# Highway FFN behind a gated recurrence: small PSUM slots for the last units, one product e for fifteen middle units, and a new order

## The chip, the core and the metric

The kernel runs on one core of a Trainium2 chip. Its engines are named as in the profile: PE (matmul), DVE (vector), ACT (activation), POOL (GpSimd) and SP, which here only starts transfers. The metric is the device time of one execution in microseconds; lower is better.

## The reference

A gated recurrence over time runs along each of 4 sequences of 6336 steps with 256 channels, and its output goes through a highway layer token by token:

```python
sig = 1.0 / (1.0 + np.exp(-f_logit))
f = lower_bound + (1.0 - lower_bound) * sig
h = f[:, t] * h + (1.0 - f)[:, t] * x[:, t]        # y[:, t] = h
...
H = np.maximum(y @ w_h, 0.0)
T = 1.0 / (1.0 + np.exp(-(y @ w_t + b_t)))
out = T * H + (1.0 - T) * y
```

All inputs and the output are float32; there are 25344 tokens (x, f_logit and the output are 26 MB each).

## The kernel before

The 25344 tokens are cut into 28 units (`parts`): two of 2 blocks of 128 tokens, one of 4, twenty-three of 8, one of 4 and one of 2. Each unit passes through a chain of steps, most of them done twice, once for each half of 128 channels. The order in which all steps of all units are issued is written out by hand as a string of tokens (lines 49 to 98). A token such as `s12.1:0` is a step (s), a unit (12), a half or part (1) and a buffer slot (0); a trailing `v` puts a step on DVE that else runs on POOL (b, e) or ACT (f, c). Every engine works through its own instructions in the order of the string, and waits by semaphores for what it reads and for a slot to be free. So an instruction that waits holds up all that stands behind it on its engine, SP's queue of transfers too.

The steps of a unit, with their engine and line:

- l, x (SP, 237): load the logits and x of the unit, 128 partitions by tokens by channels.
- u (ACT, 249): u = sigmoid(-logit), in fp16.
- b (POOL or DVE, 257): bv = u * x, in two parts, written so that two tokens make one 32-bit word.
- i (PE, 264): transposes of u into PSUM; f (ACT or DVE, 275 or 273): f = 1 + ncc * u of one half, with channels on partitions.
- p (PE, 284): transposes of bv as 32-bit words into PSUM.
- s (DVE, 301): the recurrence of one half as one scan along the tokens; it starts from the last value of the unit before, so all scans of a half run one after the other.
- z, g (PE, 313 and 115): the two matrix products of the highway layer for one half of the outputs; each reads both halves of y. t (ACT, 326): sigmoid of z. d (DVE, 330): d = max(ncc * y, g), which stands for the relu, shifted.
- e (POOL or DVE, 336): d = d * t, in parts: for a unit of 8 blocks the first half whole (1024 elements a partition) and the second in two parts of 512. A part needs d and t of the half it lies in.
- o (PE, 349 and 350): for four blocks of tokens, a product with diag and one with the identity transpose y and d back and add them; it reads both halves of d, so o.0 needs e.0 and e.1, and o.1 needs e.0 and e.2.
- c (ACT or DVE): copy of the result from PSUM; w (SP, 364): its transfer to memory.

WT, WH and dg (DVE) scale the weights and make the diagonal matrices; k is a number of idle matmuls on zeros (`k*4:1`: four, in slot 1).

PSUM has two kinds of slots. `one_bank` gives a0 and a1, one bank each, for the transposes i and p. `two_banks` gives three slots of two banks, b0 to b2, for z, g, o and k. `shared` makes every b or e on POOL wait for the b or e (or weight scaling) on DVE that was issued last before it.

Of the kernel before, what the change touches and what calls it, by code (L numbers as in the profile page):

```python
# [53 lines left out]
x7:1 f4.0:0 c1.0:1 g2.1:1 z2.0:0 p3.1:1 i4.1:0 g2.0:2 d2.1:0 s3.1 u5:0 t2.0 d2.0 f4.1:1 b4.0 w1.0 k*4:1 e2.0v e2.1v
z3.1*1:1 p4.0:1 i5.1:0 t3.1:1 b5.0:1 f5.1:2 o2.0:0 c2.0:2 w2.0 b5.1 l8:2 x8:2 g3.1:1 p4.1:0 l12:3 l10:4 z3.0:2 s4.0:1
u6:1 i5.0:1 f5.0:0 g3.0:0 x12:0 i6.1:1 x9:3 t3.0 l11:5 d3.1:0 f6.1:3 u7:0 s4.1 e3.1 p5.0:0 d3.0 z4.1:1 g4.1:0 s5.0:2
p5.1:1 i6.0:0 d4.1:1 g4.0:2 t4.1:0 f6.0:0 u9:2 z4.0:0 k*4:1 b6.1:0 i7.1:0 b6.0 e3.0 e3.2 s5.1 d4.0 b7.0:1 p6.1:1
o3.0:1 g5.1:2 t4.0 x10:4 f7.1:1 c3.0:0 w3.0 s6.1:3 i7.0:0 b7.1 z5.1:0 f7.0:2 k*4:1 d5.1:2 t5.1:1 p6.0:0 e4.1v u8:0
e4.0v o3.1:1 o4.0:0 c3.1:1 p7.1:1 z5.0:2 e5.1 g5.0:1 w3.1 c4.0:2 w4.0 t5.0 e4.2 s6.0 s7.1:0 b8.1:0 i8.1:0 z6.0:0 d5.0
f8.1:0 p7.0:1 o4.1:2 u12:1 i9.1:0 s7.0 t6.0:0 e5.2 c4.1:3 w4.1 g6.1:1 i8.0:1 u10:3 d6.1:0 g7.1:0 f8.0v:1 l27:0 z7.0:1  # L60
b8.0 p8.0:1 e5.0 t7.0:1 d7.1:1 x11:1 f9.1:2 s8.0:1 z6.1:2 g6.0:0 g7.0:1 t6.1 b12.1:1 d7.0 d6.0 i9.0:0 p8.1:1 u11:0
z7.1:2 k*4:1 b9.0:2 f9.0:1 t7.1 o5.1:1 b9.1 i11.1:0 c5.1:0 w5.1 b10.0:0 o5.0:0 f11.1:3 s8.1 c5.0:1 z8.0:2 p9.0:1 w5.0
l13:1 e7.1v g8.1:1 e6.0v i10.1:0 t8.0:2 e6.2v f10.1:0 o6.1:0 z8.1:2 e6.1v e7.0v s9.0:2 e7.2 c6.1:2 w6.1 p9.1:0 i12.1:1
t8.1 f12.1:1 o7.1:0 c7.1:3 b12.0 g8.0:2 b10.1 d8.1:2 s9.1 o7.0:1 d8.0 p10.1:1 i10.0:0 w7.1 s10.1:0 o6.0:0 e8.1 g9.0:2
u27:2 c7.0:0 f10.0:2 c6.0:1 u13:3 b11.0:2 g9.1:1 d9.0:0 p10.0:0 s10.0 w7.0 i11.0:1 b11.1 f11.0:0 z9.1:0 t9.1:0 e8.2
e8.0 z9.0:2 t9.0 i12.0:1 d9.1 f12.0:2 p11.1:0 z10.0:0 t10.0:1 e9.0 g10.0:1 l15:0 u15:0 o8.1:2 p11.0:1 s11.1:3 c8.1:0
d10.0:1 o8.0:0 c8.0:2 e9.2 e9.1v g10.1:1 i13.0:0 x15:0 o9.0:2 w6.0 x13:2 e10.0v f13.0:3 b15.0:0 z10.1:0 c9.0:1 p12.0:0
t10.1 s11.0 d10.1 i13.1:1 b15.1 z11.1:2 g11.1:1 s12.0:1 f13.1:0 t11.1:0 b13.0:2 i15.0:1 f15.0:2 l14:2 e10.1 u14:1
b13.1 p12.1:0 o9.1:0 c9.1:3 g11.0:2 i15.1:1 e10.2 l17:3 d11.1:2 s12.1 z11.0:1 t11.0 f15.1:1 x14:3 p13.0:0 z12.1:0
t12.1:1 g12.1:1 u17:0 d11.0 p13.1:1 w8.0 o10.0:2 z12.0:0 e11.1 s13.0:2 d12.1:0 b14.1:1 o10.1:1 c10.0:2 i14.0:0 g12.0:2  # L70
s13.1 b14.0 w8.1 t12.0 i14.1:1 w9.0 e11.0v w9.1 g13.0:0 c10.1:0 l16:0 e11.2v z13.0:1 x16:0 d12.0 f14.0:0 f14.1:3
d13.0:1 p14.0:0 t13.0:0 o11.1:2 s14.0:0 u16:1 l18:1 c11.1:1 e12.2 z13.1:0 p14.1:1 o11.0:1 p15.0:0 s14.1 c11.0:3 t13.1
z14.1:2 s15.0:3 g13.1:1 x17:1 d13.1 t14.1:2 g14.1:0 d14.1:2 i16.0:1 z14.0:2 e12.0 e12.1 p15.1:0 e13.0 b16.0:1 s15.1
u18:3 b16.1 w10.0 o12.0:1 f16.0:0 i16.1:1 g14.0:0 t14.0 d14.0 c12.0:2 b17.0:2 b17.1 w10.1 e13.1v f16.1:2 w11.1 o12.1:2
c12.1:0 z15.1:1 e14.0v w11.0 p16.0:0 s16.0:1 e14.2 i17.1:1 o13.0:0 t15.1:1 g15.1:1 f17.1:1 p16.1:1 d15.1:0 z15.0:2
s16.1 l20:0 c13.0:1 i18.0:0 g15.0:0 d15.0 e13.2 o13.1:1 e14.1 e15.2 u20:1 f18.0:0 x18:2 t15.0 i17.0:0 f17.0:2 b18.1:0
w12.0 p17.1:1 o14.0:2 l19:1 s17.1:2 g16.0:0 c13.1:2 p17.0:0 d16.0:1 b18.0 s17.0 o14.1:1 i18.1:1 u19:0 c14.1:3 g16.1:0
d16.1 w12.1 f18.1:1 c14.0:0 z16.1:1 t16.1:0 p18.1:1 s18.1:0 i19.0:0 z17.1:2 x20:0 e15.1 l22:2 g17.1:0 e15.0 d17.1:2
x19:1 b20.0:1 g17.0:1 f19.0:2 d17.0 b20.1 t17.1:1 b19.0:2 i19.1:0 z17.0:2 p18.0:1 u22:3 w13.1 f19.1:1 w13.0 b19.1
w14.1 s18.0 e17.1v t17.0 e17.0v o15.0:0 w14.0 e17.2 o15.1:1 c15.0:1 x22:2 i20.1:0 z16.0:2 f20.1:3 l21:0 p19.0:1 t16.0  # L80
e16.0 c15.1:0 z18.0:0 s19.0:3 b22.0:0 e16.1 b22.1 p19.1:0 o17.0:2 t18.0:1 o17.1:1 c17.0:2 i20.0:1 x21:3 g18.0:0 e16.2
s19.1 f20.0:0 c17.1:3 u21:0 b21.1:2 l23:1 g19.0:2 p20.1:0 d18.0:0 b21.0 i22.0:1 g19.1:0 f22.0:1 d19.0:2 s20.1:2
z19.0:1 d19.1 w15.1 z19.1:2 i21.0:1 p20.0:0 t19.0:2 g18.1:1 s20.0 t19.1 u23:1 w17.1 d18.1 e19.0v o16.0:0 c16.0:0 e19.1
o16.1:2 i21.1:0 f21.0:0 w15.0 f21.1:2 g20.1:0 d20.1:1 e18.0v z18.1:1 e19.2 w17.0 c16.1:1 i22.1:1 x23:0 f22.1:3 p21.1:0
o19.0:0 l24:2 t18.1 z20.1:2 b23.1:1 e18.1 e18.2 b23.0 p21.0:1 c19.0:2 o19.1:1 w16.0 t20.1:0 w16.1 e20.2 s21.1:1 s21.0
g20.0:0 c19.1:3 i23.0:0 x24:1 f23.0:2 z20.0:2 t20.0 e20.1 p22.1:1 d20.0 e20.0 z21.0:1 t21.0:1 u24:0 i23.1:0 g21.1:0
w19.0 o18.0:2 s22.1:3 c18.0:0 b24.0:2 w19.1 f23.1:0 p22.0:1 d21.1:2 b24.1 z21.1:1 t21.1 e21.2 s22.0 x25:2 g21.0:0
o18.1:2 c18.1:1 p23.0:0 d21.0 i24.1:1 s23.0:0 z22.1:1 f24.1:1 g22.1:0 l25:0 o20.0:2 e21.0 t22.1:0 p23.1:0 d22.1:0
i24.0:1 e21.1 c20.0:2 f24.0:2 o20.1:1 c20.1:3 u25:0 b25.1:0 g22.0:0 w18.0 s23.1 p24.0:1 w18.1 d22.0 l26:1 s24.0:2
z22.0:2 w20.0 z23.0:1 b25.0 t22.0 o21.1:0 p24.1:0 t23.0:1 c21.1:0 g23.1:2 i25.0:1 e22.2 s24.1 o21.0:1 f25.0:0 g23.0:0  # L90
d23.1:1 i25.1:0 d23.0 c21.0:1 p25.0:1 z23.1:1 s25.0:1 g24.1:2 u26:1 f25.1:1 t23.1 z24.1:0 e22.0 i26.1:0 d24.1:2 e22.1
w20.1 o22.1:1 x27:0 t24.1:2 c22.1:2 p25.1:1 o22.0:0 x26:1 b26.1:1 f26.1:0 c22.0:3 g24.0:2 i26.0:0 z24.0:1 s25.1 w21.1
b26.0 p26.0:1 e23.2 w21.0 f26.0:2 d24.0 z25.0:0 p26.1:0 e23.0 z25.1:2 t24.0 s26.0:3 s26.1 g25.1:1 t25.0:0 b27.0:0
# [311 lines left out]
```

## Time and profile before

| | |
|---|---|
| median of three runs | 210.59 us (209.63 to 212.25) |
| profiled execution | 211.79 us, of which the span from first to last instruction is 209.6 us |
| granted PE clock, mean | 0.998 |
| busy, of the span | PE 93%, DVE 93%, ACT 92%, POOL 83% |
| moved by DMA | 78.67 MB, mean 375 GB/s |

Busy time is the time in which an engine had an instruction in work. Matmuls overlap, so a busy PE isn't PE at its peak. In a row of the timeline stand start, duration, engine, line and operation, and in brackets the idle time before it with what ended it. In a row of groups stand the number of instructions, their busy time together, the mean of one in ns, and the idle time before them. Neighbouring instructions overlap at their ends by about 0.1 us, so the distance from start to start is what one costs in a full stretch.

### The profile page before, as it was taken

What the parts mean: (1) busy time and instruction counts of PE and PEld (TensorE: products, weight loads), DVE (VectorE), ACT (ScalarE), POOL (GpSimd) and SP (SyncE); (2) the same over time, 40 slices, a digit from 0 to 9 for tenths busy, and PEclk for the clock granted to TensorE, in tenths of its full rate; (3) what the DMA queues carried; (4) which work ended last, traced back from release to release, by engine and by line L of the source; (5) the groups of instructions that cost most, each with busy time, mean ns of one, the idle gap of its engine ahead of it and who ended that gap; (6) DMA issues with size and microseconds to landing.
All of it is one profiled execution on the core that took longest, in us unless ns stands there. A gap on an engine that the chain in (4) does not pass through costs nothing. (4 is left out here: it accounts for less than half of the span.)

```text
span 209.6 us, 4674 instructions
## 1 busy us (share of the span) xinstructions
PE 194.3 (93%) x1852; PEld 135.3 (65%) x1852; DVE 194.5 (93%) x167; ACT 192.8 (92%) x187; POOL 173.1 (83%) x114
## 2 busy tenths in 40 slices
...
GB/s 197 400 431 419 417 414 422 417 424 410 422 410 420 376 368 336 428 422 415 413 417 422 419 410 425 406 430 425 404 427 375 371 374 377 308 106 200 103 358 292
DMA packets 15980, 78.67 MB, mean 375 GB/s; under 512 B 1748, under 2 KB 2264, under 8 KB 10072
## 3 DMA queue, kind: packets, MB, share of 16 engines
...
## 5 line engine op out<-in xcount | busy, mean ns | idle before, releaser
L257 POOL TENSOR_TENSOR bv<-u,x 128x1024 bf16<-128x1024 f16 (+1 forms) x50 | 101.9, 2059 | 17.4 <-ACT u L249 8.0
L301 DVE TENSOR_TENSOR_SCAN y<-f,y,bT 128x1024 bf16<-128x1024 f16 (+5 forms) x54 | 106.9, 1990 | 1.8 <-ACT t L326 1.0
L336 POOL TENSOR_TENSOR d<-d,t 128x512 bf16<-128x512 bf16 (+2 forms) x53 | 71.4, 1364 | 12.9 <-DVE d L336 10.2
L330 DVE SCALAR_TENSOR_TENSOR d<-y,ncc,g 128x1024 bf16<-128x1024 bf16 (+2 forms) x56 | 63.2, 1137 | 2.3 <-PE g L313 1.3
L326 ACT ACTIVATE t<-z,bt 128x1024 bf16<-128x1024 f32 (+2 forms) x56 | 58.4, 1058 | 2.0 <-PE z L313 1.0
L275 ACT ACTIVATE f<-uT,ncc 128x1024 f16<-128x1024 f16 (+2 forms) x51 | 55.5, 1097 | 1.0 <-PE uT L264 1.0
L249 ACT ACTIVATE u<-l 128x2048 f16<-128x2048 f32 (+2 forms) x28 | 49.0, 1750 | 6.9 <-DMA l<-in_f_logit_dram 6.9
L359 ACT COPY o<-op 128x1024 f32<-128x1024 f32 (+1 forms) x50 | 50.7, 1025 | 2.2 <-PE op L350 2.2
L349 PE MATMUL op<-diag,y 128*128 128x128 f16 x396 | 49.4, 219 | 0.7 <-DVE d L330 0.6
L350 PE MATMUL op<-ident_b,d 128*128 128x128 bf16 x396 | 49.4, 219 | 0.1
L350 PEld LDWEIGHTS <-d 128*128 128x128 bf16 x396 | 44.1, 113 | 3.3 <-POOL d L336 0.7
L349 PEld LDWEIGHTS <-y 128*128 128x128 bf16 x396 | 44.2, 113 | 2.0
L313 PE MATMUL g<-y,w_sb 128*128 128x512 bf16 (+1 forms) x112 | 39.5, 367 | 1.2 <-ACT o L359 0.7
L313 PE MATMUL z<-y,w_sb 128*128 128x512 bf16 (+1 forms) x112 | 39.4, 367 | 1.0 <-DVE y L301 0.8
L115 PE MATMUL z<-y,w_sb 128*128 128x512 bf16 x92 | 34.9, 379 | 0.0
L115 PE MATMUL g<-y,w_sb 128*128 128x512 bf16 x92 | 34.9, 379 | 0.0
L284 PE MATMUL bT<-ident_f,bv 128*128 128x128 f32 x198 | 31.5, 276 | 3.4 <-POOL bv L257 1.4
L264 PE MATMUL uT<-ident_h,u 128*128 128x128 f16 x396 | 30.8, 219 | 3.7 <-ACT f L275 1.9
L264 PEld LDWEIGHTS <-u 128*128 128x128 f16 x396 | 25.9, 98 | 11.7 <-issue 4.9
L313 PEld LDWEIGHTS <-w_sb 128*128 128x128 f16 x224 | 21.5, 98 | 15.7 <-issue 0.9
L284 PEld LDWEIGHTS bT<-ident_f,bv 128*128 128x128 f32 x198 | 22.9, 141 | 12.4 <-POOL bv L257 2.5
L115 PEld LDWEIGHTS <-w_sb 128*128 128x128 f16 x184 | 18.0, 98 | 17.2 <-issue 3.1
...
## 6 DMA issues: line engine op xcount, KB each, us to landing
...
out_dram<-o SPq DMA_DIRECT2D x3, 256.0 KB, 14.0
```

The source lines that it names most:

```text
L115: return pe.add_instruction(mybir.InstMatmult(name=nc.get_next_instruction_name(), start_tensor_calc=start, stop_tensor_calc=stop, tile_si ...
L257: shared(pin(e.tensor_mul(st[n]["bv"][:, a:c].rearrange("p k d j -> p k j d"), st[n]["u"][:, 2 * a:2 * c].rearrange("p (k j) d -> p k j d" ...
L264: pin(nc.tensor.transpose(uT[:, j * P:(j + 1) * P], st[n]["u"][:, j, h * P:(h + 1) * P], ident_h))
L275: pin(nc.scalar.activation(to, of, AF.Identity, scale=ncc[:, h:h + 1], bias=1.0))
L284: pin(nc.tensor.transpose(words[:, k:k + g * (P - 1) + 1:g], pair, ident_f))
L301: pin(nc.vector.tensor_tensor_scan(y[:, c:e], st[n]["f", h][:, c:e], st[n]["bT", h][:, c:e], 0.0 if fresh else carry[h], op0=ALU.mult, op1 ...
L313: pin(nc.tensor.matmul(p[:, a:e], w, half(n, "y", ki)[:, a:e], start=ki == 0, stop=ki == NH - 1))
L326: pin(nc.scalar.activation(half(n, "t", m), st[n]["z", m][:, :tokens(n)], AF.Sigmoid, bias=bt[:, m:m + 1]))
L330: pin(nc.vector.scalar_tensor_tensor(half(n, "d", m), half(n, "y", m), ncc[:, m:m + 1], st[n]["g", m][:, :tokens(n)], op0=ALU.mult, op1=AL ...
L336: shared(pin(e.tensor_mul(st[n]["d"][:, a:c], st[n]["d"][:, a:c], st[n]["t"][:, a:c])), not eng)
L349: pin(nc.tensor.matmul(o, half(n, "y", h)[:, cols], diag[:, h], start=True, stop=False))
L350: pin(nc.tensor.matmul(o, half(n, "d", h)[:, cols], ident_b, start=False, stop=True))
```

## The change

Three things change. Both halves of z26, g26, z27 and g27 (the matrix products of the last two units) and the output product o27 are put into the one-bank slots a0 and a1, which until now held only transposes. For units 7 to 21, e is one product over both halves, 2048 elements a partition. And the order string is written anew: what stands on DVE, the places of loads and writes, and all slots.

In the code of o and c a part of a unit can now be narrower than four blocks, but the set of units for which it would be (`n in ()`) is empty, so these steps do what they did. The slot of the result tile is taken at the first copy.

```diff
-        units.append((nb, at, {2: (0, 1), 4: (0, 1, 2), 8: (0, 2, 4)}[nb], {2: (0, 256, 512), 4: (0, 512, 1024), 8: (0, 1024, 1536, 2048)}[nb]))
+        units.append((nb, at, {2: (0, 1), 4: (0, 1, 2), 8: (0, 2, 4)}[nb], (0, 2048) if 7 <= n <= 21 else {2: (0, 256, 512), 4: (0, 512, 1024), 8: (0, 1024, 1536, 2048)}[nb]))
...
 +l0:0 x0:0 l1:1 wt x1:1 l2:2 wh pc:0 u0:0 x2:2 k*3:1 cc l3:3 b0.0:0 u1:1 i0.0:0 x3:3 l4:0 f0.0:0 WT i0.1:1 x4:4 l5:4
+k*3:0 x5:0 k*3:0 p0.0:0 k*3:0 f0.1:1 dg p0.1:1 s0.0:0 i1.0:0 s0.1 l6:1 b1.0:1 f1.0v:0 l27:5 k*3:0 i1.1:1 z0.0:0 z0.1:1
+k*3:2 u2:0 t0.0:0 f1.1v:1 i2.0:0 k*3:0 WH i2.1:1 g0.1:0 d0.1:0 b2.1:0 f2.0:2 p1.0:0 g0.0:2 t0.1 f2.1:3 b2.0v e0.1
+k*3:1 p1.1:1 s1.0:1 s1.1 d0.0 k*3:0 p2.0:0 g1.0:0 e0.0 z1.1:1 p2.1:1 u3:1 d1.0:1 z1.0:2 t1.0:1 o0.0:0 s2.0:2 t1.1 s2.1
+g1.1:2 i3.1:0 k*3:1 c0.0:0 f3.1:0 u4:0 i3.0:1 b3.0:0 w0.0 z2.1:0 f3.0:1 b3.1v p3.1:0 k*4:1 d1.1 e1.0v e1.1 o1.0:1
+s3.1:0 c1.0:1 w1.0 x6:1 b4.1:1 l7:0 z2.0:2 p3.0:1 i4.0:0 t2.1:0 g2.0:0 s3.0 g2.1:1 d2.0:0 b4.0 x27:2 t2.0 k*3:2 f4.0:0
...
+p11.0:0 t10.1:1 z9.1:1 t10.0 s11.1:3 g10.0:0 w7.1 s11.0 i12.1:1 g10.1:2 e8.0 t9.1 x15:2 d10.0:0 d10.1 f12.1:1 b12.0
+o8.1:1 i13.1:0 u14:1 f13.1:2 b13.1:1 o8.0:0 c8.1:2 p12.1:1 b13.0 z11.1:2 i13.0:0 t11.1:0 c8.0:3 e9.0v e10.0 g11.1:1
+w8.0 b14.1:3 z11.0:2 s12.1:1 f13.0:1 t11.0 d11.1:1 p12.0:1 g11.0:0 u17:0 k*3:1 s12.0 b14.0 o9.1:1 w8.1 d11.0 e11.0
+g12.0:2 d12.0:3 i17.0:0 i14.0:1 c9.1:1 o9.0:0 w9.1 l16:0 f17.0:0 u15:3 x16:0 f14.0v:3 p13.1:0 z12.0:1 c9.0:0 w9.0
+t12.0:1 p13.0:1 b15.0:0 l18:1 z12.1:2 t12.1 o10.0:0 s13.1:2 i14.1:0 g12.1:1 f14.1:2 o10.1:2 c10.0:3 c10.1:2 s13.0
+p14.0:0 i15.0:1 b15.1 w10.1 o11.1:0 f15.0:1 x17:1 d12.1 e12.0 c11.1:1 s14.0:0 g13.0:1 w10.0 w11.1 i15.1:1 g13.1:2
+d13.0:0 u16:1 f15.1:3 p14.1:0 b16.0:1 z13.0:0 o11.0:1 d13.1 t13.0:0 c11.0:0 s14.1 w11.0 z13.1:2 l19:0 x18:2 p15.0:1
+b16.1 g14.1:0 i16.0:0 t13.1 f16.0:2 e13.0 b17.1:3 s15.0:3 z14.1:1 t14.1:1 o12.0:2 p15.1:0 g14.0:1 d14.1:1 b17.0
+c12.0:2 w12.0 p16.0:1 u18:3 s15.1 z14.0:0 t14.0 x19:0 d14.0 o12.1:2 e14.0 c12.1:3 i16.1:0 f16.1:1 z15.0:1 t15.0:0
+g15.1:0 o13.0:2 w12.1 c13.0:0 b18.0:0 s16.0:1 p16.1:0 d15.1:2 w13.0 l20:1 i17.1:1 l21:2 x20:1 g15.0:0 s16.1 b18.1
+o13.1:1 f17.1:2 d15.0 p17.0:1 p17.1:0 u19:0 s17.1:2 c13.1:1 z16.1:2 t16.1:2 s17.0 z15.1:0 w13.1 o14.0:1 t15.1 z16.0:2
+i18.0:0 g16.1:0 c14.0:2 g16.0:1 i18.1:1 w14.0 t16.0 f18.0:1 o14.1:2 f18.1:0 d16.1:0 d16.0 z17.0:0 c14.1:0 x21:3 w14.1
+p18.0:0 l22:0 i19.1:1 t17.0:1 b19.1:1 e15.0v b19.0 s18.0:0 z17.1:1 f19.1:2 t17.1 g17.0:0 u20:1 o15.0:2 c15.0:3 e16.0
+w15.0 p18.1:0 d17.0:1 b20.0:0 s18.1 p19.1:1 g17.1:0 o15.1:1 d17.1 z18.0:2 b20.1 u21:3 c15.1:1 t18.0:0 s19.1:3 i19.0:0
...
+l26:2 o21.0:0 w20.1 c21.1:2 i25.0:1 g23.0:2 i25.1:0 c21.0:3 f25.0:0 b25.0 d23.0 f25.1:1 g24.1:0 z24.0:1 u26:0 i27.1:0
+p25.0:1 z23.1:2 e22.0 f27.1:2 e22.2 x26:0 d24.1:0 o22.0:0 e23.0 p25.1:0 s25.0:2 t24.0:1 o22.1:1 w20.0 s25.1 t23.1
+z24.1:2 c22.0:0 g24.0:0 c22.1:1 d24.0 e23.2 i26.0:1 g25.0:1 d25.0:2 t24.1 i27.0:0 b26.1:0 g25.1:2 f26.0:0 f27.0:1
+d25.1 i26.1:1 b26.0 z25.0:0 w21.1 f26.1:3 p26.1:0 o23.1:1 s26.1:0 t25.0:2 e23.1 p26.0:1 e24.0 s26.0 o23.0:2 p27.1:0
+e24.2v e24.1 s27.1:3 z25.1:0 g26.0:a1 c23.1:2 w21.0 d26.0:1 o24.1:1 e25.0v w22.0 g26.1:a0 d26.1 c23.0:0 t25.1 e25.1v
+o24.0:0 c24.1:3 w22.1 w23.1 p27.0:1 z26.1:a0 s27.0 w23.0 o25.0:1 z26.0:a1 c24.0:1 t26.1:0 e25.2v t26.0 w24.1 z27.1:a0
+t27.1:1 o25.1:0 z27.0:a1 e26.1 g27.1:a0 w24.0 c25.0v:2 e26.0v c25.1:0 o26.0:1 d27.1:0 g27.0:a0 d27.0 w25.0 t27.0
+c26.0:3 e27.1 e27.0v o27.0:a0 c27.0:1 w25.1 w26.0 w27.0
...
@@ -133,7 +132,8 @@
         return t
 
     def two_banks(slot, name):
-        t = ps.tile([P, NB * P], FP32, tag=f"b{slot}", name=name)
+        one = slot[0] == "a"
+        t = ps.tile([P, 512 if one else NB * P], FP32, tag=slot if one else f"b{slot}", name=name)
         busy(t)
         return t
 
@@ -148,7 +148,7 @@
     make_identity(nc, ident_b)
 
     nc.vector.memset(zeros, 0.0)
-    once["idle"] = two_banks(2, "idle")
+    once["idle"] = two_banks("2", "idle")
     for _ in range(8):
         nc.tensor.matmul(once["idle"][:, :512], zeros[:, :P], zeros, start=True, stop=True)
 
@@ -338,30 +338,38 @@
     def blocks(n, q):
         return q * 4, min(q * 4 + 4, units[n][0])
 
-    def do_o(n, q, eng, slot):
+    def part(n, k):
+        w = 2 if n in () else 4
+        return k * w, min(k * w + w, units[n][0])
+
+    def do_o(n, k, eng, slot):
         op = two_banks(slot, "op").rearrange("p (j d) -> p j d", d=D)
-        j0, j1 = blocks(n, q)
+        a, c = part(n, k)
+        j0, j1 = blocks(n, a // 4)
         g = j1 - j0
-        for j in range(g):
-            cols = slice(j0 * P + j, j0 * P + j + g * (P - 1) + 1, g)
+        for j in range(a, c):
+            lo = j0 * P + j - j0
+            cols = slice(lo, lo + g * (P - 1) + 1, g)
             for h in range(NH):
-                o = op[:, j, h * P:(h + 1) * P]
+                o = op[:, j - a, h * P:(h + 1) * P]
                 pin(nc.tensor.matmul(o, half(n, "y", h)[:, cols], diag[:, h], start=True, stop=False))
                 pin(nc.tensor.matmul(o, half(n, "d", h)[:, cols], ident_b, start=False, stop=True))
-        st[n]["op", q] = op
-
-    def do_c(n, q, eng, slot):
-        j0, j1 = blocks(n, q)
-        o = sb([P, 4, D], FP32, "o", slot)
+        st[n]["op", k] = op
+
+    def do_c(n, k, eng, slot):
+        a, c = part(n, k)
+        j0 = a // 4 * 4
+        if ("o", j0) not in st[n]:
+            st[n]["o", j0] = sb([P, 4, D], FP32, "o", slot)
+        to, of = st[n]["o", j0][:, a - j0:c - j0], st[n]["op", k][:, :c - a]
         if eng:
-            pin(nc.vector.tensor_copy(o[:, :j1 - j0], st[n]["op", q][:, :j1 - j0]))
+            pin(nc.vector.tensor_copy(to, of))
         else:
-            pin(nc.scalar.copy(o[:, :j1 - j0], st[n]["op", q][:, :j1 - j0]))
-        st[n]["o", q] = o
+            pin(nc.scalar.copy(to, of))
 
     def do_w(n, q, eng, slot):
         j0, j1 = blocks(n, q)
-        pin(nc.sync.dma_start(rows(out, n, j0, j1), st[n]["o", q][:, :j1 - j0]))
+        pin(nc.sync.dma_start(rows(out, n, j0, j1), st[n]["o", j0][:, :j1 - j0]))
 
     here = locals()
     for token in order.split():
```

The lines left out of the new order, between units 4 and 11 and between 19 and 24, have the same steps in the same manner; e3 to e5 have two or three parts on DVE there and e17 is on DVE whole. Of the old order (lines 49 to 98) these are the first and the last lines:

```
l0:0 x0:0 pc:0 wh wt u0:0 l2:1 x1:1 l1:2 l3:3 cc x2:2 x3:3 i0.0:0 b0.0v:0 l4:0 u2:1 u1:2 x4:4 i0.1:1 f0.1v:0 k*16:1
l5:4 x5:0 WT l6:5 dg WH p0.1:1 f0.0v:1 x6:5 s0.1:0 p0.0:0 k*4:0 s0.0 i1.0:1 i1.1:0 b1.0:0 z0.0:0 f1.1v:0 g0.0:1 d0.0:0
f1.0:1 p1.1:1 l7:1 t0.0:0 z0.1:2 u3:0 p1.0:0 b2.0:0 s1.1:1 k*4:0 g0.1:0 i2.1:1 t0.1 s1.0 i3.0:0 d0.1 z1.1:0 f2.1:0
e0.0 f3.0:1 b2.1v z1.0:1 g1.0:2 i2.0:1 d1.0:1 f2.0:2 e0.1v i3.1:0 t1.0:0 p2.0:1 b3.0v:1 s2.0:2 g1.1:2 d1.1 o0.0:1 t1.1
...
d23.1:1 i25.1:0 d23.0 c21.0:1 p25.0:1 z23.1:1 s25.0:1 g24.1:2 u26:1 f25.1:1 t23.1 z24.1:0 e22.0 i26.1:0 d24.1:2 e22.1
w20.1 o22.1:1 x27:0 t24.1:2 c22.1:2 p25.1:1 o22.0:0 x26:1 b26.1:1 f26.1:0 c22.0:3 g24.0:2 i26.0:0 z24.0:1 s25.1 w21.1
b26.0 p26.0:1 e23.2 w21.0 f26.0:2 d24.0 z25.0:0 p26.1:0 e23.0 z25.1:2 t24.0 s26.0:3 s26.1 g25.1:1 t25.0:0 b27.0:0
t25.1 o23.1:0 d25.1:0 z26.1:2 e24.2 i27.0:0 c23.1:0 i27.1:1 e23.1v e24.0v f27.0v:0 g25.0:1 z26.0:0 t26.1:1 o24.1:2
w22.1 p27.0:0 f27.1:1 e24.1 p27.1:1 d25.0 t26.0 g26.0:0 o24.0:1 c24.1:1 c24.0:2 e25.1v w22.0 w23.1 e25.0v d26.0:3
w24.1 e25.2 s27.0:2 o25.0:2 w24.0 g26.1:0 e26.0 c25.0:0 o23.0:1 c23.0:3 s27.1 w25.0 g27.0:2 d26.1 o25.1:0 d27.0:1
z27.0:2 e26.1 o26.0:1 c25.1v:1 t27.0:0 w23.0 z27.1:2 e27.0 w25.1 g27.1:0 t27.1 c26.0:2 d27.1 e27.1v o27.0:0 c27.0:0
w26.0 w27.0
```

74 lines of the change are left out of this document (23 added, 51 removed).

## The prediction

> **What bounds the kernel now.** I read the page's busy times first, then the windows by stage, then the groups by shape on each engine, then the start and the end of the timeline.
>
> ```profile
> span 209.6 us, 4674 instructions
> PE 194.3 (93%) x1852; PEld 135.3 (65%) x1852; DVE 194.5 (93%) x167; ACT 192.8 (92%) x187; POOL 173.1 (83%) x114
> ```
> ```profile
> core 0: us, PE busy (x) PEld busy (x) DVE busy (x) ACT busy (x) POOL busy (x), PEclk, DMA share, GB/s
> 80.00:100.00 20.00, 18.77 (x179) 12.94 (x178) 19.01 (x14) 19.91 (x18) 17.98 (x11) 1.00 1.01 400
> 120.00:140.00 20.00, 19.59 (x195) 13.73 (x192) 20.00 (x13) 20.00 (x19) 19.84 (x12) 1.00 1.02 418
> 140.00:160.00 20.00, 19.05 (x190) 13.73 (x190) 19.44 (x17) 19.34 (x19) 16.79 (x11) 1.00 1.01 414
> 160.00:180.00 20.00, 20.00 (x200) 14.40 (x198) 19.95 (x13) 20.00 (x20) 20.00 (x13) 1.00 1.00 371
> 180.00:195.00 15.00, 14.67 (x141) 10.05 (x140) 14.63 (x10) 13.53 (x15) 15.00 (x11) 1.00 0.43 172
> ```
>
> DVE, ACT and PE are all within 2 us of each other, and in the middle DVE and ACT are full: from 80 to 160 us DVE lost 1.0 us in one window and 0.6 in another, nothing in the others shown. No engine has room in the middle; what a new order can win there is only work taken off DVE and ACT. DMA is full until the 160s and then half empty (share 0.43 at 180 to 195), so loads don't set the end. POOL has the most room over the span, but none from 160 to 195 us. DVE is therefore my ruler: the span is its 194.5 us of work plus 15.1 us in which it had none, at the start, at the end and a little between.
>
> **The work taken from DVE and ACT.** These groups give the prices.
>
> ```profile
> L301 DVE TENSOR_TENSOR_SCAN y<-f,y,bT 128x1024 bf16<-128x1024 f16 x40 | 93.1, 2336 | 1.8 <-ACT t L326 1.0 <-PE bT L284 0.5 <-issue 0.2
> L330 DVE SCALAR_TENSOR_TENSOR d<-y,ncc,g 128x1024 bf16<-128x1024 bf16 x46 | 57.4, 1258 | 1.0 <-issue 0.6 <-PE g L115 0.4
> L336 DVE TENSOR_TENSOR d<-d,t 128x1024 bf16<-128x1024 bf16 x11 | 7.7, 698 | 0.0
> L336 DVE TENSOR_TENSOR d<-d,t 128x512 bf16<-128x512 bf16 x12 | 5.1, 437 | 0.2 <-ACT t L326 0.2
> L273 DVE TENSOR_SCALAR f<-uT,ncc 128x256 f16<-128x256 f16 x4 | 1.9, 478 | 0.4 <-PE uT L264 0.4
> L257 DVE TENSOR_TENSOR bv<-u,x 128x512 bf16<-128x512 f16 x2 | 1.9, 950 | 0.0
> L257 DVE TENSOR_TENSOR bv<-u,x 128x1024 bf16<-128x1024 f16 x1 | 1.3, 1321 | 0.0
> L336 DVE TENSOR_TENSOR d<-d,t 128x256 bf16<-128x256 bf16 x3 | 0.9, 290 | 0.1
> L273 DVE TENSOR_SCALAR f<-uT,ncc 128x1024 f16<-128x1024 f16 x1 | 1.3, 1278 | 0.0
> ```
> ```profile
> L275 ACT ACTIVATE f<-uT,ncc 128x1024 f16<-128x1024 f16 x45 | 52.0, 1161 | 0.2 <-PE uT L264 0.2
> ```
>
> Products e on DVE: before 7.7 + 5.1 + 0.9 = 13.7 us. In the new order, counting the tokens that end in v, there are 4 of 1024 elements, 8 of 512, 2 of 256 and 3 of 2048 (e9, e15, e17). No row shows 2048 on DVE. Below it is bounded by 1.0 us (four times what 512 more elements cost, 698 - 437 = 261 ns), above by two of 1024, 1.4 us; I take the line through the two rows, 698 + 2 x 261 = 1.22 us, since both rows lie on it. Sum: 2.8 + 3.5 + 0.6 + 3.7 = 10.6, so 3.1 us less. Gates f on DVE: two of 256 fewer (1.0 less), two of 1024 more (2.6 more): 1.6 us more; ACT gets the opposite, two of 1161 ns fewer and two small ones more, about 1.4 us less. Products b on DVE: one of 512 fewer, about 1.0 us less. Together **DVE loses 2.5 us of work** and ACT 1.4 us. This counts in full, because both are full in the middle. Scans, gate products d and copies are the same in number on every engine; PE gets 61 idle matmuls for 49, and their 12 times 0.2 us stand at the front half of the order, where PE waits for DVE; if that cover were gone they would cost 2.6 us.
>
> **POOL: e of fifteen middle units in one product.**
>
> ```profile
> L257 POOL TENSOR_TENSOR bv<-u,x 128x1024 bf16<-128x1024 f16 x45 | 96.1, 2156 | 7.3 <-DMA x<-in_x_dram 2.7 <-ACT f L275 2.5 <-DVE bv L257 1.7
> L336 POOL TENSOR_TENSOR d<-d,t 128x512 bf16<-128x512 bf16 x38 | 43.9, 1163 | 12.0 <-DVE d L336 10.2 <-ACT o L359 1.4 <-DVE d L330 0.2
> L336 POOL TENSOR_TENSOR d<-d,t 128x1024 bf16<-128x1024 bf16 x12 | 25.6, 2136 | 0.1
> ```
>
> The step from 512 to 1024 elements is 973 ns, so 2048 is 2136 + 2 x 973 = 4.08 us (below, 3.9 for four such steps; above, 4.65 for the four 512s that it replaces; the two rows speak for the line). It replaces 2136 + 2 x 1163 = 4.46. POOL saves 0.4 us a unit, but now takes all of e in twelve of the fifteen units, where DVE had parts. Its sum rises by 2.9 us for e, and 1.2 us for a b that DVE did: 177 us. Against that it stops waiting for DVE's products: the 10.2 us are eight waits (the first row below), in which the code makes a POOL product follow the DVE product issued before it. The new order has only three such places in the middle. And POOL starts earlier (the other two rows):
>
> ```profile
> POOL d L336 <- DVE d L336: 10.2, 8, 2.5
> ```
> ```profile
> 4.80 0.72 DVE L257 TENSOR_TENSOR bv<-u,x 128x512 bf16<-128x512 f16 x1
> 10.28 1.17 POOL L257 TENSOR_TENSOR bv<-u,x 128x512 bf16<-128x512 f16 x1 [8.04 <-ACT u L249]
> ```
>
> POOL's first b waited until 10.3 us for the second unit's u; in the new order it takes b0.0, whose u DVE already used at 4.8 us. So POOL has 5 us more in front and some 7 us fewer waits for 4 us more work: in the sum over the span it hides. By stretch it is tight: a unit with b and e wholly on POOL costs 2 x 2.14 + 4.08 = 8.4 us, and DVE needs 7.0 for its two scans and two d (start to start, below). From b13 to e14 the order has five in a row: 41.8 us of POOL against 37.6 of DVE with e9.0 and f14.0.
>
> ```profile
> 163.51 2.35 DVE L301 TENSOR_TENSOR_SCAN y<-f,y,bT 128x1024 bf16<-128x1024 f16 x1
> 165.78 1.25 DVE L330 SCALAR_TENSOR_TENSOR d<-y,ncc,g 128x1024 bf16<-128x1024 bf16 x1
> 166.97 2.35 DVE L301 TENSOR_TENSOR_SCAN y<-f,y,bT 128x1024 bf16<-128x1024 f16 x1
> ```
> ```profile
> 159.32 0.44 PE bT L284 x4
> ```
>
> I walked this stretch by hand with 2.26 and 1.19 us (these starts) from the end of d8.0. POOL ends b13.0 at 10.5 us and must wait for e9.0 on DVE until 15.2; e10.0 to 19.3, b14 to 23.6, e11.0 to 27.7, b15 to 32.0, e12.0 to 36.1, b16 to 40.3, e13.0 to 44.4, b17 to 48.7. DVE reaches s17.1 at 51.5. Its eight transposes on PE take about 1 us (the last row: four start in 0.44), so 1.7 us of slack are left at the tightest place. Further on, e15.0 meets POOL 0.6 us before b19.1 ends, e17.0 just as b20.1 ends. PE stands 1 us before o13.0 and o14.0, which nothing waits for in that time. For **the middle I take 0.5 us more stall than now**; the bounds are 1.5 us less (all of what the windows show now) and, above, the 4.2 us by which POOL's stretch exceeds DVE's.
>
> One row shows the price of a collision on the port that both engines read through:
>
> ```profile
> 152.65 2.16 POOL L257 TENSOR_TENSOR bv<-u,x 128x1024 bf16<-128x1024 f16 x1
> 154.54 0.81 DVE L336 TENSOR_TENSOR d<-d,t 128x1024 bf16<-128x1024 bf16 x1
> ```
>
> DVE's product began 0.27 us before POOL's ended and took 0.81 instead of 0.70 us. The Trainium skill ("SBUF — State Buffer", section "Who interferes with whom") says that a VectorE instruction with two SBUF inputs contends with GpSimd, as an exclusive lock. By that rule all of an overlap is lost; by the row, under half of it. The overlap of e15.0 above would then cost 0.6 instead of 0.3 us.
>
> **The start.**
>
> ```profile
> 7.05 0.62 DVE L210 TENSOR_SCALAR w_sb<-w_raw,cc 128x256 f16<-128x256 f32 x2 [1.16 <-DMA w_raw<-in_moe_w_t_dram]
> 9.57 0.63 ACT L249 ACTIVATE u<-l 128x512 f16<-128x512 f32 x1 [0.24 <-DMA l<-in_f_logit_dram]
> 9.61 1.26 DVE L301 TENSOR_TENSOR_SCAN y<-f,bT 128x256 bf16<-128x256 f16 x2
> 31.28 2.34 DVE L301 TENSOR_TENSOR_SCAN y<-f,y,bT 128x1024 bf16<-128x1024 f16 x1
> ```
>
> w_t is the fourth load of SP's queue in both orders, so WT again runs at 7.05; after dg the first scan can start at about 8.3 us (f0 is now on ACT). w_h moves from third to seventh, behind 1.75 MB, where l1 stood before and landed at 9.5: WH runs at 10.4 after both f1, and d0.1 waits about 0.5 us for the g that needs it. Step by step I reach the end of s4.1 at 30.4 us; now it ends at 31.28 + 2.34 = 33.6. But now DVE has done b0.0, one more small f, e0.1, e2.0, e2.1 and d3.1 by then, 3.5 us, all counted above or merely moved; 30.4 against 30.1 is **0.3 us lost**. Bounds: 1 us won, 2 us lost, if l3, now behind x2, is late. l27 and x27 move up to behind l6 and l7: 0.5 MB in a full queue at about 400 GB/s, 1.3 us later for l7 on, which by my walk lands 2 us before u7.
>
> **The end.** g26, z26, z27, g27 and o27 move to slots a0 and a1, which the transposes leave by then.
>
> ```profile
> 188.01 2.35 DVE L301 TENSOR_TENSOR_SCAN y<-f,y,bT 128x1024 bf16<-128x1024 f16 x1 [0.37 <-PE bT L284]
> 201.67 0.48 DVE L330 SCALAR_TENSOR_TENSOR d<-y,ncc,g 128x256 bf16<-128x256 bf16 x1 [0.44 <-PE g L313]
> 202.55 1.23 DVE L357 COPY o<-op 128x1024 f32<-128x1024 f32 x1 [0.40 <-PE op L350]
> 204.24 0.48 DVE L330 SCALAR_TENSOR_TENSOR d<-y,ncc,g 128x256 bf16<-128x256 bf16 x1 [0.47 <-PE g L313]
> 205.71 0.59 ACT L359 COPY o<-op 128x512 f32<-128x512 f32 x1 [0.51 <-PE op L350]
> ```
>
> From 180 us on DVE loses 0.37 + 0.44 + 0.40 + 0.47, and 0.3 before its last product: 2.0 us, mostly for the small products that queue for the three wide slots. Walking the new end from the start of s26.1, I still find two waits: d27.1 0.4 us for t27.1 to empty a0, and d27.0 0.75 us, since o26.0 (sixteen matmuls, waiting for e26) stands ahead of g27.0 in PE's queue. **0.9 us won**; bounds 0 and 2.0. From the last copy's end (206.3) to the span's end are 3.3 us of the last write, which stays.
>
> Sum: -2.5 + 0.3 + 0.5 - 0.9 = -2.6 us. ACT by the same steps (1.4 less work, about 2 us less idle at the end, which is now 4) would end earlier, so DVE decides. The profiled execution took 211.8 us, 2.2 beyond its span, so 209.2; it was 1.2 us above the median shown, and **I forecast 208.0 us** on the median's level.
>
> **Rivals.** First, the gain is whole: no stall in the middle (-1.0), the start 0.5 us better, all 2.0 of the end: -2.5 - 0.5 - 2.0 - 1.0 = -6.0, or 204.6. For it: e17.0 meets POOL's gap within 0.1 us in my walk, so the order fits these durations. Against it: o26.0 before g27.0. Second, on the slower side, POOL becomes the bound: if POOL arrives at b13 more than 1.7 us late (its b waits for x, or 2048 costs more than the line), DVE waits at s17, and in both stretches of full POOL units (10 to 14, 18 to 22) the 8.4 against 7 us shows in full, 4.2 + 4.5. With the other terms (-3.1) +5.6: 216.2. For it: POOL is full from 160 to 195 us already now; against it: its lead of some 5 us at 10 us. Third, the collision: only the POOL product ahead in the order can be in flight, a b of 2.14 us, at e9, e15 and e17; if DVE stood for the whole of each, +6.4 - 3.1: 213.9. For it: the collision row, which shows a loss at all; against it: in my walk POOL stands before e9.0 and is at an end at the others. (The rule of the Trainium skill named above would make each such meeting a full wait.) Fourth, the small slots do nothing, as ACT's copies set the end: -1.7, 208.9, inside the forecast.
>
> **Chances.** Within 2% (about what a measurement of this kernel can tell from no change), the forecast with the fourth: 0.42. Whole gain: 0.36. POOL as the bound: 0.16, the collisions 0.06, both slower by over 2% or close to it: 0.22. The range reaches from 203.6 (the first rival and one more us) to 214.4 (the third, and the lesser half of the second). The likeliest one's own range is 206.4 to 211.
>
> **What would show it.** DVE's busy time near 192 us and ACT's near 191.4; POOL near 177 with under 4 us of waits for DVE's e; POOL's 2048 near 4.08 us; the first scan near 8.3; in the last 10 us DVE waits below 1.3 us. I am wrong if scans wait for transposes behind POOL's b between units 13 and 23, if DVE's e of 2048 take over 2 us, or if ACT waits for l from u7 on.

## The result, and the profile after

The changed kernel takes 209.01 us (208.51 to 209.53, 14 runs), the kernel before 210.62 us in runs on the same chip (209.63 to 212.62, 14 runs): ratio 0.9912, 95% interval 0.9891 to 0.9933. That is 1.6 us less, within 2%. The forecast was 208.0.

First the two opening lines of the page after.

```profile
span 207.1 us, 4655 instructions
PE 196.7 (95%) x1835; PEld 136.3 (66%) x1864; DVE 193.0 (93%) x157; ACT 191.8 (93%) x187; POOL 176.9 (85%) x94
```

The span is 2.5 us shorter than in the profiled execution before, 1.5 of it busy time of DVE. The windows of three stages (start, middle, end; columns as in the prediction) show the rest: after, then before, then the kernel of the ninth experiment, whose order is that of before up to the last ten us.

```profile
0.00:40.00 40.00, 37.70 (x279) 22.81 (x285) 31.75 (x43) 31.87 (x36) 26.41 (x28) 1.00 0.97 385
40.00:180.00 140.00, 136.43 (x1322) 97.07 (x1342) 139.72 (x92) 138.82 (x127) 133.51 (x56) 1.00 1.01 408
180.00:215.00 35.00, 22.60 (x237) 16.44 (x239) 21.54 (x24) 21.10 (x26) 16.95 (x12) 0.94 0.44 174
```
```profile
0.00:40.00 40.00, 33.93 (x249) 20.31 (x250) 32.77 (x45) 31.40 (x34) 24.39 (x25) 1.00 0.97 388
40.00:180.00 140.00, 135.76 (x1340) 96.85 (x1339) 138.40 (x100) 139.11 (x129) 128.33 (x75) 1.00 1.01 405
180.00:215.00 35.00, 24.61 (x267) 18.09 (x265) 23.34 (x24) 22.31 (x26) 20.35 (x16) 0.95 0.47 186
```
```profile
40.00:180.00 140.00, 136.54 (x1353) 97.27 (x1352) 139.59 (x100) 139.39 (x130) 129.84 (x76) 1.00 1.01 407
```

DVE's idle time is the stage's length less its busy time. Start: 7.2 before, 8.25 after, so 1.0 lost. Middle: 1.6 and 0.3, so 1.3 won. End, up to the end of the span (29.6 and 27.1 us long): 6.3 and 5.6, so 0.7 won. With the 1.5 of work that makes -2.5. But the third fence says that 1.2 of the middle's 1.3 wasn't won by the change: the same order in another execution stood idle for 0.4 us there. The profiled execution before was 1.2 us above its median, and this stall is where. What the change gives on the span is then -1.5 + 1.0 - 0.1 - 0.7 = -1.3 us. The runs agree: the median span is 208.4 us in 62 runs of the kernel before and 207.2 in the 14 after. The single terms are good to some 0.4 us only: in the execution of the third fence DVE had 194.9 us of work instead of 194.5, and in experiments 1 to 3 and 8, whose start is that of after, DVE's idle time there is 7.8 to 8.6.

The other 0.3 lie outside the span. The time is 2.15 us longer than the span in the 62 runs before, 2.16 in experiment 9 and 2.22 in experiment 2; it is 1.77 to 1.84 in every kernel with merged products e, experiment 10 among them (medians). So this part goes with the merged products; why, no run shows.

These groups after answer to the prices of the prediction, and POOL's waits from 30 to 190 us (total, times, longest) to its row of eight.

```profile
L336 DVE TENSOR_TENSOR d<-d,t 128x2048 bf16<-128x2048 bf16 x3 | 4.3, 1422 | 0.0
L336 DVE TENSOR_TENSOR d<-d,t 128x1024 bf16<-128x1024 bf16 x4 | 2.7, 687 | 0.1
L336 DVE TENSOR_TENSOR d<-d,t 128x512 bf16<-128x512 bf16 x8 | 3.3, 420 | 0.0
L273 DVE TENSOR_SCALAR f<-uT,ncc 128x1024 f16<-128x1024 f16 x3 | 3.8, 1273 | 0.1
L336 POOL TENSOR_TENSOR d<-d,t 128x2048 bf16<-128x2048 bf16 x12 | 49.1, 4088 | 1.2 <-DVE d L336 1.2
```
```profile
POOL bv L257 <- DVE d L336: 6.0, 4, 2.5
POOL d L336 <- DVE d L336: 1.2, 1, 1.2
```

POOL's product of 2048 costs 4.09 us, the line's 4.08. DVE's costs 1.42 instead of 1.22, since POOL was in work at the start of each (the last section has one alone). Start and end after:

```profile
8.59 1.41 DVE L301 TENSOR_TENSOR_SCAN y<-f,bT 128x256 bf16<-128x256 f16 x2
12.89 0.48 DVE L330 SCALAR_TENSOR_TENSOR d<-y,ncc,g 128x256 bf16<-128x256 bf16 x1 [1.10 <-PE g L313]
26.37 4.58 DVE L301 TENSOR_TENSOR_SCAN y<-f,y,bT 128x1024 bf16<-128x1024 f16 x2
36.74 6.82 DVE L301 TENSOR_TENSOR_SCAN y<-f,y,bT 128x1024 bf16<-128x1024 f16 x3
198.93 1.22 DVE L366 COPY o<-op 128x1024 f32<-128x1024 f32 x1 [0.27 <-PE op L356]
200.97 0.48 DVE L330 SCALAR_TENSOR_TENSOR d<-y,ncc,g 128x256 bf16<-128x256 bf16 x1 [0.43 <-PE g L313]
202.02 0.48 DVE L330 SCALAR_TENSOR_TENSOR d<-y,ncc,g 128x256 bf16<-128x256 bf16 x1 [0.56 <-PE g L313]
```
```profile
201.84 1.01 ACT L368 COPY o<-op 128x1024 f32<-128x1024 f32 x1
203.60 0.59 ACT L368 COPY o<-op 128x512 f32<-128x512 f32 x1 [0.74 <-PE op L356]
```

The first scan runs at 8.6, a microsecond earlier than before, but d0.1 waits 1.1 us for its g. At the end DVE's waits are 0.27 + 0.43 + 0.56 = 1.3 us, and the last copy ends at 204.2 instead of 206.3.

### The profile page after: what moved, and what is told of

Same layout as the page of the kernel before. It is cut to its first block, busy times and chain, and to the rows that moved or that the text cites. A ratio compares the mean times of both kernels' runs of the same rounds, so it can differ in the third digit from the quotient of the medians.

```text
span 207.1 us, 4655 instructions
## 1 busy us (share of the span) xinstructions
PE 196.7 (95%) x1835; PEld 136.3 (66%) x1864; DVE 193.0 (93%) x157; ACT 191.8 (93%) x187; POOL 176.9 (85%) x94
## 4 chain that ended last, share of the span: by engine, by line
PE 71%; DVE 10%; DMA 9%; issue 3%; ACT 2%; POOL 2%; SPq 0%; ACTq 0%; DVEq 0%; POOLq 0%
PE z L313 9%; PE g L313 9%; PE op L356 9%; PE op L355 9%; PE bT L284 9%; PE uT L264 8%; PE g L114 8%; PE z L114 7%; DVE y L301 7%; DMA x<-in_x_dram 7%; DMA l<-in_f_logit_dram 2%; DVE d L330 2%; POOL bv L257 2%; PE idle L114 1%; DVE d L336 1%
## 5 line engine op out<-in xcount | busy, mean ns | idle before, releaser
L257 POOL TENSOR_TENSOR bv<-u,x 128x1024 bf16<-128x1024 f16 (+1 forms) x51 | 103.1, 2049 | 14.1 <-DVE d L336 6.0
L336 POOL TENSOR_TENSOR d<-d,t 128x512 bf16<-128x512 bf16 (+3 forms) x32 | 74.0, 2322 | 10.7 <-DVE d L336 4.1
L326 ACT ACTIVATE t<-z,bt 128x1024 bf16<-128x1024 f32 (+2 forms) x56 | 57.3, 1058 | 1.6 <-PE z L313 1.0
L275 ACT ACTIVATE f<-uT,ncc 128x1024 f16<-128x1024 f16 (+2 forms) x51 | 53.8, 1065 | 2.7 <-PE uT L264 2.2
L313 PE MATMUL z<-y,w_sb 128*128 128x512 bf16 (+1 forms) x108 | 38.0, 367 | 0.7
L114 PE MATMUL g<-y,w_sb 128*128 128x512 bf16 x84 | 31.8, 379 | 0.1
L114 PE MATMUL z<-y,w_sb 128*128 128x512 bf16 x79 | 29.9, 379 | 0.2
```

The costliest lines, as they stand in the source:

```text
L114: return pe.add_instruction(mybir.InstMatmult(name=nc.get_next_instruction_name(), start_tensor_calc=start, stop_tensor_calc=stop, tile_si ...
L257: shared(pin(e.tensor_mul(st[n]["bv"][:, a:c].rearrange("p k d j -> p k j d"), st[n]["u"][:, 2 * a:2 * c].rearrange("p (k j) d -> p k j d" ...
L275: pin(nc.scalar.activation(to, of, AF.Identity, scale=ncc[:, h:h + 1], bias=1.0))
L313: pin(nc.tensor.matmul(p[:, a:e], w, half(n, "y", ki)[:, a:e], start=ki == 0, stop=ki == NH - 1))
L326: pin(nc.scalar.activation(half(n, "t", m), st[n]["z", m][:, :tokens(n)], AF.Sigmoid, bias=bt[:, m:m + 1]))
L336: shared(pin(e.tensor_mul(st[n]["d"][:, a:c], st[n]["d"][:, a:c], st[n]["t"][:, a:c])), not eng)
```

## The experiments

Each undoes or adds one thing; ratios are to the kernel before, in brackets the 95% interval. "Against after" compares medians of different sessions, in which the kernel before took 210.3 to 210.7 us: a few tenths of such a difference can be noise.

**1. Small slots undone.** The order after, with the products of the last two units in the wide slots.

```diff
-g26.0:a1 o24.1:1 g26.1:a0 o24.0:0 z26.1:a0 o25.0:1 z26.0:a1 z27.1:a0 z27.0:a1 g27.1:a0 o26.0:1 g27.0:a0 o27.0:a0
+g26.0:1 o24.1:2 g26.1:0 o24.0:1 z26.1:2 o25.0:0 z26.0:1 z27.1:2 z27.0:1 g27.1:2 o26.0:0 g27.0:1 o27.0:2
```

> The changed kernel with one thing undone: g26, z26, z27, g27 and o27 go through the three two-bank slots again, in the same order of steps. The changed kernel took 209.0 us, and DVE waited 1.3 us in its last 10 us for small products. Theory (the slots are worth the end's gain): DVE waits at least 2 us there again and the time is 209.6 to 210.6 us. Rival (ACT's copies set the end, the slots are worth nothing): 208.7 to 209.3 us, with the last copy at the same distance from the last scan.

210.60 us, 0.9999 (0.9979 to 1.0019): the whole gain is gone. Its end:

```profile
201.75 0.48 DVE L330 SCALAR_TENSOR_TENSOR d<-y,ncc,g 128x256 bf16<-128x256 bf16 x1 [1.16 <-PE g L313]
203.66 0.48 DVE L330 SCALAR_TENSOR_TENSOR d<-y,ncc,g 128x256 bf16<-128x256 bf16 x1 [1.43 <-PE g L313]
205.24 0.59 ACT L368 COPY o<-op 128x512 f32<-128x512 f32 x1 [0.74 <-PE op L356]
```

The two waits are 1.16 + 1.43 instead of 0.43 + 0.56, 1.6 us more, and the time is 1.6 us more. In this order the small slots are worth 1.6 us.

**2. Three parts of e again**, on the same engine, one behind the other.

```diff
-(0, 2048) if 7 <= n <= 21 else {2: ...
+{2: ...
-e10.0
+e10.0 e10.1 e10.2      (and so for units 7 to 21)
```

> The changed kernel with e of units 7 to 21 in three parts again (1024, 512, 512), one after the other at the same place of the order and on the same engine. POOL gets 2144 + 2 x 1166 - 4088 = 0.39 us more in each of twelve units, 4.7 in all. Theory (POOL's sum hides, only the stretch from b13 to e14 is tight, with 1.7 us of slack against 1.9 more work): 209.0 to 209.6 us, DVE's idle time between 40 and 180 us below 0.8 us. Rival (one long product is what took the middle's stalls of 1.3 us away): 210.2 us or more, with scans waiting for transposes behind POOL's b.

213.31 us, 1.0148 (1.011 to 1.0186): 4.3 us more than after, so POOL's 3.4 us more don't hide. The rival's number came, but not by its waits: from 30 to 180 us the scans wait only 0.6 us for transposes. DVE's busy time is 195.7, 2.7 more than after; this is DVE's group in it:

```profile
L337 DVE TENSOR_TENSOR d<-d,t 128x1024 bf16<-128x1024 bf16 x7 | 7.4, 1054 | 0.1
```

At 687 ns each, seven would take 4.8. POOL comes late, its b is still running when DVE begins an e, and DVE's product is stretched (the last section has the rows): 2.6 us of the 4.3. DVE's idle time is 1.5 us more.

**3. All e on POOL.**

```diff
-e9.0v ... e15.0v ... e17.0v
+e9.0 ... e15.0 ... e17.0
```

> The changed kernel with e9, e15 and e17 on POOL instead of DVE: DVE loses three products of 1.4 us (some 1.3 each from start to start), POOL gets three of 4.1. Theory (DVE is the ruler but POOL has only a little slack in a stretch): of the 3.9 us that DVE wins, e9 gives its 1.3, since POOL waits there now; behind e15 and e17 POOL is late for b20 and b21, DVE waits 2 to 4 us, and the time is 207.7 to 209.7 us. Rival A (POOL hides wholly, DVE is the only ruler): 205.1 to 205.6 us. Rival B (POOL is the bound): 211 us or more.

217.86 us, 1.0352 (1.0315 to 1.0388). Theory and Rival A are out; Rival B, POOL as the bound, holds. It is the second rival of the prediction; a window and the waits it foretold:

```profile
120.00:140.00 20.00, 16.62 (x159) 11.45 (x157) 15.63 (x10) 18.35 (x18) 20.00 (x9) 1.00 1.02 422
```
```profile
DVE y L301 <- PE bT L284: 7.5, 7, 2.5
PE op L356 <- POOL d L336: 6.7, 5, 2.4
```

POOL is full, DVE's scans wait 7.5 us for transposes behind POOL's b. Moving 4.3 us of e off DVE, at 12.3 us of POOL, costs 8.9 us against after.

**4. Three f on ACT.**

```diff
-f9.0v:0 ... f14.0v:3 ... f22.0v:1
+f9.0:0 ... f14.0:3 ... f22.0:1
```

> The changed kernel with f9.0, f14.0 and f22.0 on ACT instead of DVE: DVE loses three of 1.27 us (1.2 from start to start, 3.5 in all), ACT gets three of 1.0 from start to start. Theory (DVE and ACT are both full in the middle, and ACT with three more sets the end): ACT's 3.0 us less the 1 us in which it stands idle between 20 and 180 us, so 210.5 to 212.2 us, and DVE shows idle time of 4 us or more. Rival (DVE alone is the ruler): 205.4 to 206.5 us.

213.80 us, 1.018 (1.0148 to 1.0212). 3.1 us more on ACT (194.9 busy) cost 4.8, more than the theory allowed; DVE has 2.9 less to do and doesn't profit:

```profile
140.00:160.00 20.00, 16.64 (x176) 12.09 (x175) 16.72 (x13) 17.88 (x18) 17.54 (x8) 1.00 1.01 409
```
```profile
DVE d L330 <- PE g L114: 4.5, 3, 3.2
PE g L313 <- ACT o L368: 2.6, 1, 2.6
```

No engine is full there: a product g waits for a copy on ACT, and DVE's d for g.

**5 and 6. Less work on one engine.** First POOL: e of units 11, 14 and 20 over half its elements.

```diff
-(0, 2048) if 7 <= n <= 21 else {2: ...
+(0, 1024) if n in (11, 14, 20) else (0, 2048) if 7 <= n <= 21 else {2: ...
```

> The changed kernel (209.0 us) with e11, e14 and e20 done only over the first 1024 of 2048 elements (half of the product is left out): POOL loses 1.95 us three times, 5.8 in all, and nothing else changes. The runs before this one showed that 3.4 us more on POOL cost 4.3 us, and 3.0 us more on ACT 4.8. Theory (POOL, DVE and ACT are each full in the middle, so work added to any of them shows and work taken from one of them doesn't): 208.6 to 209.2 us, POOL idle some 6 us longer. Rival (POOL alone sets the pace and DVE follows): 203.5 to 205.5 us.

Then DVE:

```diff
-c8.0:3 e9.0v e10.0 ... b19.1:1 e15.0v b19.0 ... p19.0:0 e17.0v b21.1:3
+c8.0:3 e10.0 ... b19.1:1 b19.0 ... p19.0:0 b21.1:3
```

> The changed kernel with e9, e15 and e17, the three products of 2048 elements on DVE, left out. DVE loses 3.9 us (1.3 each from start to start) and POOL its three waits of 1.2 us for them, 3.6 in all; ACT keeps all its work. Theory (three full engines): ACT, which has 1.0 us idle between 20 and 180 us, lets only 0.5 to 1.5 us through: 207.5 to 208.5 us, with DVE idle 2.5 us or more in the middle. Rival (DVE and POOL set the pace, ACT follows): 205.0 to 206.0 us.

208.14 us, 0.9886 (0.9848 to 0.9924), and 208.36 us, 0.9896 (0.9866 to 0.9927). 5.8 us less on POOL give 0.9, a little more than the theory had, 3.5 us less on DVE (busy 189.5) give 0.65. So work taken away from POOL or DVE gives under a fifth of itself (the intervals overlap that of after, so even this little is barely clear of noise), while work added to POOL or ACT cost more than itself (2 and 4): several engines are at their limit together. Less work on ACT alone was not run.

**12. Less work on all three**: 6 without those e on DVE, and less t (ACT) and e (POOL) in units 11, 14 and 20.

```diff
-e9.0v ... e15.0v ... e17.0v
-        pin(nc.scalar.activation(half(n, "t", m), st[n]["z", m][:, :tokens(n)], AF.Sigmoid, ...))
+        w = 384 if n in (11, 14, 20) else tokens(n)
+        pin(nc.scalar.activation(half(n, "t", m)[:, :w], st[n]["z", m][:, :w], AF.Sigmoid, ...))
+        if n in (11, 14, 20):      (in e)
+            c = 384
```

> The changed kernel with less work on all three engines at once: e9, e15 and e17 are left out (DVE 3.9 us less), and of units 11, 14 and 20 the sigmoid t is taken over the first 384 of 1024 elements of each half (ACT about 3.5 us less) and the product e over the first 384 of 2048 (POOL about 9 us less). Taking work from POOL alone gave 0.9 us, from DVE and POOL 0.7. Theory (the three engines are the bound together, and nothing else is): 205.2 to 206.3 us. Rival (PE, which stands idle only 0.3 us in 20, or the loads, are a fourth bound): 207.2 to 208.4 us.

207.70 us, 0.9883 (0.9841 to 0.9924): DVE 189.9, ACT 189.5, POOL 167.8, all 2 to 9 us lighter, and 1.3 us come through, as the rival had it: something beside these three holds. A window of the middle, and the waits of DVE and ACT that grew:

```profile
140.00:160.00 20.00, 19.76 (x210) 14.64 (x208) 19.00 (x14) 19.25 (x20) 18.17 (x8) 1.00 1.02 421
```
```profile
DVE y L301 <- PE bT L284: 1.6, 2, 0.9
ACT o L371 <- PE op L359: 1.4, 5, 0.4
```

PE is nearly full while the other three have idle time; from 30 to 180 us it waits 0.7 us in all, and DVE and ACT wait for it. That makes PE the likely fourth bound, but a busy PE isn't PE at its peak, and the DMA queues are full too (share 1.02), so which of the two holds isn't shown.

**7. Fewer idle matmuls.** After, these rows stand on PE ahead of the g for which d0.1 waits:

```profile
11.60 0.38 PE L125 MATMUL idle<-zeros 128*128 128x512 bf16 x1
11.81 0.59 PE L114 MATMUL idle<-zeros 128*128 128x512 bf16 x2
```

```diff
-z0.1:1 k*3:2 u2:0 ... i2.0:0 k*3:0 WH
+z0.1:1 u2:0 ... i2.0:0 WH
```

> The changed kernel without two groups of three idle matmuls: the one before i2.0 and the one before i2.1, both at 10.7 to 12.3 us on PE, ahead of the g that DVE waits 1.1 us for at 12.9 us. Theory (the idle matmuls in PE's queue, not WH, are what g waits for): that wait falls to 0.4 to 0.6 us and DVE's first scan of unit 1 starts 0.6 us earlier; of it 0.2 to 0.6 us arrive at the end, 208.4 to 208.8 us. Rival (g waits for WH, or the full engines behind take the gain): the time stays at 208.9 to 209.2 us; if PE's granted clock falls without them, it is longer.

208.99 us, 0.9943 (0.9914 to 0.9972).

```profile
11.31 0.48 DVE L330 SCALAR_TENSOR_TENSOR d<-y,ncc,g 128x256 bf16<-128x256 bf16 x1 [0.18 <-PE g L313]
11.71 1.41 DVE L257 TENSOR_TENSOR bv<-u,x 128x512 bf16<-128x512 f16 x1
17.50 1.72 DVE L257 TENSOR_TENSOR bv<-u,x 128x1024 bf16<-128x1024 f16 x1
36.30 6.82 DVE L301 TENSOR_TENSOR_SCAN y<-f,y,bT 128x1024 bf16<-128x1024 f16 x3
```

The wait falls from 1.10 to 0.18 (0.18 in experiment 11 too), so the idle matmuls caused it: 0.92 us won. But DVE's two products b now begin while POOL has one in work, and take 1.41 and 1.72 us instead of 0.73 and 1.29 after: 1.1 us lost. That DVE is still 0.44 us ahead at 36 us (36.74 after) comes from w_t, which landed 0.66 us earlier in this execution (WT at 6.68, after 7.34). Of this lead 0.3 reach the end of the span (206.8). The median is that of after, but it says little: six runs took 208.4 to 208.8, one 209.2 and five 210.1 to 210.8, and no run shows what parts them.

**8. g27 ahead of o26** in PE's queue.

```diff
-g27.1:a0 w24.0 c25.0v:2 e26.0v c25.1:0 o26.0:1 d27.1:0 g27.0:a0 d27.0
+g27.1:2 w24.0 c25.0v:2 e26.0v c25.1:0 g27.0:a0 o26.0:1 d27.1:0 d27.0
```

> The changed kernel with g27.1 in slot b2, which is free there, instead of a0, and g27.0 ahead of o26.0 in PE's queue. Theory (d27.1 waits for the slot that t27.1 empties, d27.0 for the sixteen matmuls of o26.0): DVE's two waits of 0.43 and 0.56 us before them fall to under 0.2 each and the last copy starts 0.5 to 0.8 us earlier: 208.2 to 208.6 us. Rival (ACT's last copies set the end): 208.8 to 209.2 us.

209.07 us, 0.9922 (0.9892 to 0.9953), the rival's number.

```profile
201.04 0.87 DVE L330 SCALAR_TENSOR_TENSOR d<-y,ncc,g 128x256 bf16<-128x256 bf16 x2 [0.43 <-PE g L313]
202.12 1.65 ACT L368 COPY o<-op 128x1024 f32<-128x1024 f32 x2 [0.16 <-ACT t L326]
```

The second wait is gone and the last copy ends 0.4 us earlier (203.77), but the copy of o26, whose write is twice as big as the last, starts 0.3 later, and the span is 207.4. What ends it is the queue of writes: after, the last write lands 2.0 us after its issue, the least of all 51, and here, behind that of o26, no write lands in under 2.6. The windows from 204 to 206 us, before, after and in this kernel:

```profile
204.00:206.00 2.00, 0.98 (x10) 0.47 (x8) 0.77 (x2) 1.49 (x3) 0.00 (x0) 1.00 1.02 403
```
```profile
204.00:206.00 2.00, 0.00 (x0) 0.00 (x0) 0.00 (x0) 0.18 (x1) 0.00 (x0) 0.66 0.86 334
```
```profile
204.00:206.00 2.00, 0.00 (x0) 0.00 (x0) 0.00 (x0) 0.00 (x0) 0.00 (x0) 0.75 0.98 384
```

**11. Start and end together**: the deletions of 7, and

```diff
-g27.1:a0 ... w25.0 t27.0 c26.0:3 e27.1
+g27.1:2 ... w25.0 c26.0:3 t27.0 e27.1
```

> The changed kernel without the two groups of idle matmuls before i2.0 and i2.1, with g27.1 in slot b2 and with c26.0 ahead of t27.0 on ACT, so that the copy behind the last large write starts earlier. Theory (the end is set by the last writes, 0.5 MB of w26 behind c26.0, at 400 GB/s): c26.0 starts 0.3 to 0.5 us earlier, and with it the time falls to 208.3 to 208.8 us. Rival (the chain through the last copy c27.0 sets the end): 208.9 to 209.3 us.

209.74 us, 0.9964 (0.9935 to 0.9993); neither number was hit.

```profile
201.61 1.01 ACT L368 COPY o<-op 128x1024 f32<-128x1024 f32 x1 [0.31 <-PE op L356]
204.03 0.58 ACT L368 COPY o<-op 128x512 f32<-128x512 f32 x1 [1.03 <-issue]
```

The copy of o26 is 0.2 us earlier, but t27.0 now stands behind it and the last copy is 0.4 later. Each of the two shifts the other; no version with all its work has a median clearly below that of after.

**9 and 10. One part alone on the old order.** First the small slots, in the order before:

```diff
-g27.0:2 z27.0:2 z27.1:2 g27.1:0 o27.0:0
+g27.0:a0 z27.0:a1 z27.1:a1 g27.1:a0 o27.0:a0
```

> The kernel before (210.5 us), with one thing done: g27, z27 and o27 go through the one-bank slots a0 and a1, where they are free in its order (z26 and g26 can't, since a0 and a1 hold transposes of unit 27 there until after them). In its profile DVE waited 2.0 us in the end, and the writes ran at full rate from 202 us to the end. Theory (the slots shorten DVE's waits, but the writes that stand in a queue set the end): 209.6 to 210.4 us. Rival (the slots are worth here what undoing them cost in the changed kernel, 1.6 us): 208.6 to 209.2 us.

Then one product e for units 8, 12, 15, 16, 20 and 21, at the place of the last part, on POOL:

```diff
-{2: (0, 1), ...}[nb], {2: (0, 256, 512), ...
+{2: (0, 1), ...}[nb], (0, 2048) if n in (8, 12, 15, 16, 20, 21) else {2: (0, 256, 512), ...
```

> The kernel before (210.5 us), with e in one product of 2048 elements for the six units whose three parts are all on POOL there (8, 12, 15, 16, 20, 21), at the place of the last part. POOL saves 0.28 us in each from start to start, 1.7 in all; DVE and ACT keep their work. Theory (DVE and ACT are full in that order too, so POOL's gain doesn't show, and o of those units comes later): 210.0 to 211.2 us. Rival (one long product is a gain by itself): 208.8 to 209.4 us.

210.75 us, 1.0016 (0.9985 to 1.0048), and 211.66 us, 1.0048 (1.0016 to 1.008). Neither gains in the old order; both came out above the range of their theory, the second a little slower than the kernel before. Both are partial, as z26 and g26 stayed in wide slots and only six units were merged. With 1 and 2 they say that the gain needs the slots, the products and the order together; the new order with neither was not run.

## Why the forecast was near, and where its steps failed

**The level.** The sum was -2.6 us against the profiled execution, and that execution's span did fall by 2.5. But it was laid on the median, 1.2 us lower, as if all of the old stall had been the kernel's. The row of the middle in the ninth experiment shows that this execution had 1.2 us of stall of its own. Against a usual execution, the change gave -1.3 on the span. The terms missed by +1.0 (work), +0.7 (start), +0.2 (end) and -0.6 (middle), together +1.3, and 0.3 were won outside the span. So that the forecast was only 1.0 us too low is in part luck: 0.9 us of errors the other way.

**Work on DVE, forecast -2.5, measured -1.5.** By the sum of durations the step was right: e 13.7 to 10.9, f 3.2 to 4.7, b 3.2 to 2.0, together -2.5. The error is in pricing by duration: with 157 instructions instead of 167, the overlaps of neighbours (sum of durations less busy time) fall from 11.9 to 11.0 us, so ten instructions less save some 0.9 less than their durations. (An e of 512 has 420 ns, and the next instruction starts 0.33 after it.)

**POOL hides in the sum: wrong.** POOL's busy time (176.9) and its three waits at e9, e15 and e17 (1.2 for e, 1.16 and 1.21 for b) were as foretold. But the "some 7 us fewer waits" didn't come: over the whole span POOL waits 4.1 us in e and 6.0 in b for products e on DVE, 10.1 instead of 10.2. The prediction counted the waits of e alone. Nor did the 5 us in front: POOL's first b runs at 4.3 us, but then POOL waits 3.4 and 2.0 us for the diagonals and weights that DVE prepares, and by 40 us it has done 2.0 us more work than before (26.41 for 24.39). And the sum over the span is no measure: from 60 to 190 us POOL stands idle only for the three waits, and experiment 2 shows that 3.4 us more work cost 4.3. The walk had 4.7 us of waiting at e9.0; it was 1.2, so POOL's lead was mis-sized by 3.5 us.

**Middle, forecast +0.5, measured -0.1** once the stall of that execution is set aside: no scan waits for POOL. The walk's 1.7 us of slack held.

**Start, forecast +0.3, measured +1.0.** The scan came at 8.6 instead of 8.3, since w_t landed 0.3 us later than before (WT at 7.34 for 7.05). The wait of d0.1 was put at 0.5 and is 1.1, and the step left out the six idle matmuls ahead of g in PE's queue. s4.1 ends at 26.37 + 4.58 = 30.95 instead of 30.4.

**End, forecast -0.9, measured -0.7.** Both waits found in the walk are there (0.43 and 0.56 for 0.4 and 0.75). "3.3 us of the last write, which stays" failed as a rule: from the end of the last copy to the span's end are 2.9 us after, 3.6 in experiment 8 and 3.0 in 11, so a write ahead of the last one sets the end too.

**Rivals.** The whole gain didn't come: the start lost and the end kept two waits. POOL as the bound didn't come, but experiment 3 shows it one step away: 8.9 us. The collision came in small (below). That the slots do nothing is refuted here, and true in the old order for those that fit there.
